# Attention products of a fused attention and two-expert-layer kernel, taken as 64x64 quarters of TensorE's array

## The chip, the cores and the metric

The kernel runs on one core of a Trainium2 chip. The metric is the device time of one execution in microseconds (us); the median of three runs of the kernel before is 707.98 us (705.53 to 710.4). The engines are named as in the profile: PE (TensorE matmuls), PEld (TensorE weight loads), DVE (VectorE), ACT (ScalarE), POOL (GpSimd) and SP (SyncE, which issues most DMAs).

## What is computed

Three stages follow one another: an attention with a decaying state, and two layers that send every token to one of eight experts. Only the first is touched by the change.

```python
f = 1.0 / (1.0 + np.exp(-f_logit))            # q, k, v, f_logit: (4, 8, 768, 48)
for t in range(S):
    state = f[:, :, t, :, None] * state + np.einsum('bhd,bhe->bhde', k[:, :, t], v[:, :, t])
    y[:, :, t] = np.einsum('bhd,bhde->bhe', q[:, :, t], state)
...
x = attn_out.transpose(0, 2, 1, 3).reshape(B * S, H * D)     # 3072 tokens of 384
x = _moe_ref(x=x, **moe_kwargs)                               # first expert layer, with a capacity
return _moe2_ref(x=x, **moe2_kwargs)                          # second expert layer
```

## The kernel before

**Tiles.** The 3072 tokens are cut into 24 tiles of 128 tokens, six to a batch. Within a tile the recurrence is turned into matrix products: cumulative sums of the log gates (`G`, L402) give growth and decay factors `eg` and `ei`, the queries and keys are scaled by them (`QT` L422, `KD` L424), and each half tile of 64 tokens needs a product of scores (`sc`, L444), a masked copy of them (`SC`, L449), an update of the 48x48 states of all heads (`kv`, L466, summed into `S` at L478, and scaled to the next tile's start at L487), and an output (`y`, L509) from the state and from the masked scores. The eight heads lie as four pairs: one head of a pair on partitions 0 to 63, the other on 64 to 127.

**How the products use the array.** The scores are 16 products a tile on two quarters of the array: rows 0 to 63 with output partitions 0 to 63, and rows 64 to 127 with 64 to 127. The state updates are 8 products a tile with all 128 rows and 64 output partitions, 96 columns wide: for the first half tile the values stand in a buffer `Vn` whose lower 64 partitions are a copy (`copy_v`, L372) and whose upper ones are zero. The output is 16 products a tile, again 128 rows by 64 output partitions and 96 columns, and needs its operands block-wise: ACT places the state into a buffer `RS` with zero blocks (`place`, L498 and L499), and `RV` holds the values in the same manner; half of it comes by two DMAs of its own (`load_vs`, 2 x 48 KB a tile, L367 and L368), the other half by copies on POOL and DVE (`copy_vs`, L379). Each product in fp32 shows as two weight loads and two matmuls in the trace, transposes as one.

**Order of the work.** A software pipeline is written as a table `STAGES` of (stage, lag): in iteration `it` each stage works on tile `it - lag`, in the order of the table, and each engine takes its instructions in that order. On PE a tile's turn is `G`, `sc`, `kv`, the transposes `xp` (of output rows, L530) and `kp` (of keys, L433), `y`, and the router logits `rt` (L260), with some steps of the router (L131 to L141, L266) at every third tile. After the loop the last tiles are written out by hand, with pieces of the first expert group (L1140, L1163) between them, up to the sorting of the experts by their counts, which begins with a product `ps` (L802). The expert layers follow.

**Buffers and loads.** PSUM has eight 2 KB banks: `sc` and the `tr` tiles (`G`, `kp`, `xp`) and `rt` have two buffers each, `kv` and `y` one. SP issues, a tile, `F` (gates, 192 KB), two halves of `X` (keys and queries, 192 KB each), `Vn` (192 KB) and the two `RV` loads, and besides the stores of output rows (582 KB at every third tile), some weights for the first expert (`raw`, 256 KB each) and two clears of tables. `gates` (L392, L393) is on ACT, `bound` (L386) clips the gates on DVE before it. POOL also subtracts split weights (L1026) and issues the scatters of the router (L273).

Of the kernel before, what the change touches and what calls it, by code (L numbers as in the profile page):

```python
# [9 lines left out]
F32 = mybir.dt.float32  # L10
# [5 lines left out]
ALU = mybir.AluOpType  # L16
# [6 lines left out]
DM = H * D  # L23
# [3 lines left out]
P = 128  # L27
# [172 lines left out]
def _route(*args, **kw):  # L200
# [14 lines left out]

STAGES = (
    ("place", 6),
    ("bound", 2),
    ("g_choose", 9),
    ("g_save", 13),  # L220
    ("sums", 3),
    ("rows", 7),
    ("warm", 0),
    ("load_v", 3),
    ("load_vs", 4),
    ("load_x", 0),
    ("copy_v", 4),
    ("scores", 4),
    ("masked", 4),
    ("expand", 3),  # L230
    ("updates", 5),
    ("copy_vs", 5),
    ("g_rank", 10),
    ("g_store", 10),
    ("g_copy", 8),
    ("gates", 2),
    ("rows_t", 7),
    ("factors", 3),
    ("rows_c", 7),
    ("keys_t", 4),  # L240
    ("output", 6),
    ("g_list", 13),
    ("states", 5),
    ("lead", 11),
    ("g_turn", 8),
# [59 lines left out]
def _attention(tc, env, fn, kq, vn, vs, x1, tab1, early, masks, first, side, after, first_group):  # L305
# [3 lines left out]
    with ExitStack() as ctx:  # L309
# [10 lines left out]
        mask = env.cs[:, C_MASK : C_MASK + 64].unsqueeze(1).to_broadcast([P, 8, 64])  # L320
# [4 lines left out]
        NVB = 3  # L325
        NXB = 4
        NRB = 3
# [4 lines left out]
        vbuf = [b1.tile([P, 2, DM], F32, name=f"Vn{i}") for i in range(NVB)]  # L332

        sbuf = [b1.tile([P, 2, 2, NPAIR * D], F32, name=f"RS{i}") for i in range(2)]
        rbuf = [b1.tile([P, 2, 2, NPAIR * D], F32, name=f"RV{i}") for i in range(NRB)]
# [6 lines left out]
        for vb in vbuf:  # L342
            nc.gpsimd.memset(vb[64:128, 0], 0.0)
        for r in rbuf + sbuf:
            nc.gpsimd.memset(r[0:64, :, 1, :], 0.0)
            nc.gpsimd.memset(r[64:128, :, 0, :], 0.0)
# [11 lines left out]
        def load_v(i):  # L358
            t = tiles[i]
            t.Vn = vbuf[i % NVB]  # L360
            nc.sync.dma_start(out=t.Vn[:, 1], in_=vn[i])

        def load_vs(i):

            t = tiles[i]
            t.RV = rbuf[i % NRB]
            nc.sync.dma_start(out=t.RV[0:64, 1, 0, :], in_=vs[i, 0])  # L367
            nc.sync.dma_start(out=t.RV[64:128, 0, 1, :], in_=vs[i, 1])  # L368

        def copy_v(i):  # L370
            t = tiles[i]
            nc.gpsimd.tensor_copy(out=t.Vn[0:64, 0], in_=t.Vn[0:64, 1])  # L372

        def copy_vs(i):

            t = tiles[i]
            for h in range(2):
                u = slice(h * 64, h * 64 + 64)
                (nc.vector if h else nc.gpsimd).tensor_copy(  # L379
                    out=t.RV[u, h, h].rearrange("p (a e) -> p a e", e=D),  # L380
                    in_=t.Vn[u, 1].rearrange("p (a h e) -> p a h e", h=2, e=D)[:, :, h],
                )
# [35 lines left out]
        def factors(i):  # L418
            t = tiles[i]
            t.QT = b4.tile([P, NPAIR, P], F32, name=f"QT{i}", tag="QT")  # L420
            t.KD = e2.tile([P, NPAIR, P], F32, name=f"KD{i}", tag="KD")
            nc.vector.tensor_tensor(out=t.QT, in0=t.X[:, 1], in1=t.eg, op=ALU.mult)  # L422
            step()
            nc.vector.scalar_tensor_tensor(  # L424
# [12 lines left out]
        def scores(i):  # L437
            t = tiles[i]
            sc = t.sc = p_2.tile([P, NPAIR, 2, 64], F32, name=f"sc{i}", tag="sc")
            for a in range(NPAIR):  # L440
                for h in range(2):
                    u = slice(h * 64, h * 64 + 64)
                    for q in (slice(0, 64), slice(64, 128)):
                        nc.tensor.matmul(sc[q, a, h], t.KD[q, a, u], t.QT[q, a, u], start=True, stop=True)  # L444
# [1049 lines left out]
def tile_attention_moe_moe(  # L1494
# [91 lines left out]
    with ExitStack() as mo:  # L1586
# [22 lines left out]
        def side(i):  # L1609
# [12 lines left out]
            if i == SNAP + 14:  # L1622
                M.index(g0)
# [178 lines left out]
```

## Time and profile before

| | |
|---|---|
| median of 3 runs | 707.98 us |
| profiled execution, its own time | 709.22 us |
| its span, first to last instruction | 707.4 us |
| PE busy | 676.5 us (96% of the span) |
| DVE, ACT, POOL busy | 409.8, 322.2, 361.2 us |
| mean granted TensorE clock | 0.991 |
| attention loop, from the sums of tile 4 to those of tile 23 | 25.31 to 143.95 us |
| sorting of the first layer's experts begins | 177.95 us |

The span is one execution seen by the profiler; 1.8 us of the execution's own time lie outside of it. A matmul's row gives when it started and a modelled end, so the pace of PE is read from start to start. A group's mean duration is not its pace: matmuls overlap.

### The profile page before, as it was taken

To read this page: it belongs to the slowest core of one execution; us is meant where nothing else is said; L and a number is where in the kernel's file an instruction comes from. 1 tells how busy PE (TensorE), PEld (TensorE's weight loads), DVE (VectorE), ACT (ScalarE), POOL (GpSimd) and SP (SyncE) were. 2 spreads that over 40 slices of the span, in tenths; PEclk is the share of its full clock that TensorE was granted. 3 is DMA by queue.
4 is the path that set the end of the run, shared out by engine and by line. 5 is a ranking of instruction groups with operands and counts; after the bars stand their busy time and mean duration, and the time that the engine had idled before them with its cause. 6 is when DMAs were issued, how large, how long until landed. Compare 5 with 4: busy or idle time off the path is not lost.

```text
span 707.4 us, 15778 instructions
## 1 busy us (share of the span) xinstructions
PE 676.5 (96%) x5775; PEld 619.0 (87%) x5778; DVE 409.8 (58%) x1024; ACT 322.2 (46%) x697; POOL 361.2 (51%) x389
## 2 busy tenths in 40 slices
PE   7989999989999999999999899989999999999995
PEld 4878788877898989989999899989998899999994
DVE  4767777866486555745546654456344455464641
ACT  5668777743353434344343433144334334354420
POOL 5233444454365546565473651456656464576621
PEclk9999999999999999999999999999999999999998
DMA  8899899532485545355473520275445354454300
GB/s 191 248 203 224 199 183 215 127 83 93 131 258 159 152 120 155 97 154 141 126 185 97 159 95 1 68 237 161 141 115 164 101 155 131 136 154 147 92 25 20
DMA packets 63273, 99.79 MB, mean 141 GB/s; under 512 B 16588, under 2 KB 32942, under 8 KB 63187
## 3 DMA queue, kind: packets, MB, share of 16 engines
q1 hardware_dynamic: 55507, 83.06, 44.0%
q0 software_dynamic: 7680, 15.64, 7.9%
q8 instruction: 47, 0.77, 0.5%
q14 instruction: 39, 0.32, 0.2%
HBM read 82.90 MB, written 16.60 MB: 141 GB/s over the span
## 4 chain that ended last, share of the span: by engine, by line
PE 72%; DVE 9%; DMA 8%; issue 5%; ACT 2%; POOL 1%; SPq 0%; DVEq 0%; POOLq 0%; ACTq 0%
PE hpm L1163 27%; PE ypm L1187 8%; PE ypm L1188 8%; PE ypm L1189 8%; DMA out_dram<-yr,tdm 6%; PE y L509 3%; PE G L402 3%; PE sc L444 3%; PE tpm L1140 2%; PE kv L466 1%; PE tym L926 1%; PE warm L629 1%; PE tym L1001 1%; PE ltm L260 1%; PE kp L433 1%
## 5 line engine op out<-in xcount | busy, mean ns | idle before, releaser
L1174 ACT ACTIVATE hhm<-hpm 128x288 fp32r<-128x288 f32 (+11 forms) x152 | 72.4, 477 | 184.0 <-PE hpm L1163 163.5
L1163 PE MATMUL hpm<-xhm,w0h 128*128 128x288 f32 (+11 forms) x456 | 155.2, 341 | 0.4 <-DVE hlm L1175 0.3
L1187 PE MATMUL ypm<-hhm,w1h 128*128 128x288 f32 (+11 forms) x456 | 153.9, 338 | 0.0
L1175 DVE SCALAR_TENSOR_TENSOR hlm<-hpm,hhm 128x288 fp32r<-128x288 f32 (+11 forms) x152 | 81.2, 536 | 120.9 <-ACT hhm L1174 92.6
L1188 PE MATMUL ypm<-hlm,w1h 128*128 128x288 f32 (+11 forms) x456 | 150.6, 330 | 0.0
L1163 PE MATMUL hpm<-xhm,w0l 128*128 128x288 f32 (+11 forms) x456 | 150.5, 331 | 0.0
L1189 PE MATMUL ypm<-hhm,w1l 128*128 128x288 f32 (+11 forms) x456 | 150.4, 330 | 0.0
L1163 PE MATMUL hpm<-xlm,w0h 128*128 128x288 f32 (+11 forms) x456 | 144.6, 331 | 0.0
L1026 POOL TENSOR_TENSOR w0l<-raw,w0h 128x512 fp32r<-128x512 f32 x64 | 81.9, 1296 | 57.9 <-ACT w0h L1025 57.5
L1026 POOL TENSOR_TENSOR w1l<-raw,w1h 128x512 fp32r<-128x512 f32 x64 | 82.1, 1295 | 41.5 <-ACT w1h L1025 40.6
L295 POOL DMA_INDIRECT xrm<-x,idcm x64 | 69.8, 1090 | 55.6 <-DVE valm L1021 34.0
L1163 PEld LDWEIGHTS hpm<-xhm,w0h 128*128 128x128 f32 x456 | 86.3, 189 | 3.6 <-DVE hlm L1175 1.0
L1187 PEld LDWEIGHTS ypm<-hhm,w1h 128*128 128x128 f32 x456 | 85.9, 188 | 2.8 <-issue 0.6
L1163 PEld LDWEIGHTS hpm<-xhm,w0l 128*128 128x128 f32 x456 | 86.4, 190 | 2.0
L1189 PEld LDWEIGHTS ypm<-hhm,w1l 128*128 128x128 f32 x456 | 85.9, 188 | 2.2
L1188 PEld LDWEIGHTS ypm<-hlm,w1h 128*128 128x128 f32 x456 | 86.0, 189 | 2.1
L1163 PEld LDWEIGHTS hpm<-xlm,w0h 128*128 128x128 f32 x456 | 85.2, 189 | 2.3
L273 POOL DMA_INDIRECT tab<-pos,sum x30 | 30.5, 1018 | 64.8 <-DVE sum L182 58.4
L1148 ACT CAST xhm<-tpm 128x336 fp32r<-128x336 f32 (+8 forms) x64 | 25.2, 435 | 72.1 <-PE tpm L1140 69.0
L1025 ACT CAST w0h<-raw 128x512 fp32r<-128x512 f32 x96 | 57.2, 616 | 0.1
L1025 ACT CAST w1h<-raw 128x512 fp32r<-128x512 f32 x96 | 56.7, 621 | 0.0
L1149 DVE TENSOR_TENSOR xlm<-tpm,xhm 128x336 fp32r<-128x336 f32 (+8 forms) x64 | 29.4, 493 | 42.1 <-ACT xhm L1148 41.2
(209 smaller groups left out, 1040.4 us busy)
## 6 DMA issues: line engine op xcount, KB each, us to landing
raw<-in_w_dram SPq DMA_DIRECT2D x192, 256.0 KB
X<-in_kq_dram SPq DMA_DIRECT2D x48, 192.0 KB
x<-xr SPq DMA_DIRECT2D x8, 582.0 KB
F<-in_fn_dram SPq DMA_DIRECT2D x24, 192.0 KB
Vn<-in_vn_dram SPq DMA_DIRECT2D x24, 192.0 KB
RV<-in_vs_dram SPq DMA_DIRECT2D x48, 48.0 KB
xrm<-x,idcm POOLq DMA_INDIRECT x64
tab<-fill SPq DMA_DIRECT2D x2, 480.0 KB
```

Of the source, the lines that this page charges most:

```text
L273: ins = tc.nc.gpsimd.indirect_dma_start(out=dst, out_offset=bass.IndirectOffsetOnAxis(ap=idx, axis=0), in_=src, in_offset=None, bounds_che ...
L295: nc.gpsimd.indirect_dma_start(out=dst, out_offset=None, in_=src, in_offset=bass.IndirectOffsetOnAxis(ap=idx, axis=0), bounds_check=bound, ...
L1025: nc.scalar.copy(out=hi, in_=raw)
L1026: eng.tensor_tensor(out=lo, in0=raw, in1=hi.bitcast(F32), op=ALU.subtract)
L1148: nc.scalar.copy(out=g.xh[:, :, s], in_=tp[:, :, :Pr])
L1149: nc.vector.tensor_tensor(out=g.xl[:, :, s], in0=tp[:, :, :Pr], in1=g.xh[:, :, s].bitcast(F32), op=ALU.subtract)
L1163: nc.tensor.matmul(hp[:, :N], w[:, c, fs], x[:, c, :N], start=(k == 0), stop=(k == len(parts) - 1))
L1174: nc.scalar.activation(hh[:, :N], hp[:, :N], AF.Relu)
L1175: nc.vector.scalar_tensor_tensor(out=hl[:, :N], in0=hp[:, :N], scalar=0.0, in1=hh[:, :N].bitcast(F32), op0=ALU.max, op1=ALU.subtract)
L1187: nc.tensor.matmul(g.yp[d][:, :N], w2h[:, fc, ds_], hh[:, :N], start=(fc == 0), stop=False)
L1188: nc.tensor.matmul(g.yp[d][:, :N], w2h[:, fc, ds_], hl[:, :N], start=False, stop=False)
L1189: nc.tensor.matmul(g.yp[d][:, :N], w2l[:, fc, ds_], hh[:, :N], start=False, stop=(fc == NFC - 1))
```

## The change

The three kinds of products are written as 64x64 quarters, and everything that only fed their block form is dropped. `load_vs`, `copy_v`, `copy_vs` and `place` are gone, with the buffers `RV`, `RS` and the memsets of their zeros. `output` becomes `output_s` (queries times state, read from `S` itself) and `output_i` (masked scores times values, read from `Vn` itself). The states are added in two instructions, and the scaling of the state and `bound` move from DVE to POOL. `factors` is split into `queries` and `keys`. In PSUM `sc` and `kv` now share one buffer of two banks, one bank for each half of the array's rows, and take it one after the other within a tile; `y` has two banks. The values get four buffers.

```diff
 def scores(i):
-    sc = t.sc = p_2.tile([P, NPAIR, 2, 64], F32, name=f"sc{i}", tag="sc")
+    t.sc = p_1.tile([P, 2, 512], F32, name=f"sc{i}", tag="sc")
     for a in range(NPAIR):
-        for h in range(2):
-            u = slice(h * 64, h * 64 + 64)
-            for q in (slice(0, 64), slice(64, 128)):
-                nc.tensor.matmul(sc[q, a, h], t.KD[q, a, u], t.QT[q, a, u], start=True, stop=True)
+        for h, q in enumerate(half):
+            for u in half:
+                nc.tensor.matmul(
+                    t.sc[u, h, a * 64 : a * 64 + 64], t.KD[q, a, u], t.QT[q, a, u], start=True, stop=True
+                )
...
 def updates(i):
-    t.kv = p_1.tile([P, NPAIR, 2, D], F32, name=f"kv{i}", tag="kv")
+    t.kv = p_1.tile([P, 2, 512], F32, name=f"kv{i}", tag="sc")
...
-            nc.tensor.matmul(
-                t.kv[q, a, 0:n], t.KT[:, a, q], t.Vn[:, 0:n, v0 : v0 + D], start=True, stop=True
-            )
+            for k, u in enumerate(half[:n]):
+                nc.tensor.matmul(
+                    t.kv[q, k, a * D : (a + 1) * D],
+                    t.KT[u, a, q],
+                    t.Vn[u, v0 : v0 + D],
+                    start=True,
+                    stop=True,
+                )
...
 def states(i):
-    nc.vector.tensor_tensor(
-        out=t.S[:, 1:n].rearrange("p h (a e) -> p h a e", a=NPAIR),
-        in0=t.kv[:, :, 0 : n - 1].rearrange("p a h e -> p h a e"),
-        in1=pair(t.S[:, 0]).unsqueeze(1).to_broadcast([P, n - 1, NPAIR, D]),
-        op=ALU.add,
-    )
-    step()
+    for k in range(2 if c < TPB - 1 else 1):
+        nc.vector.tensor_tensor(
+            out=t.S[:, k + 1], in0=t.kv[:, k, 0 : NPAIR * D], in1=t.S[:, k], op=ALU.add
+        )
+        step()
     if c < TPB - 1:
-        nc.vector.tensor_tensor(
+        nc.gpsimd.tensor_tensor(
             out=pair(S[:, 0]),
...
-def output(i, pool=p_1, tag="y"):
-    t.y = pool.tile([P, 512], F32, name=f"y{i}", tag=tag)
...
-                nc.tensor.matmul(
-                    t.y[u, 2 * a * D : (2 * a + 2) * D].rearrange("p (h e) -> p h e", h=2),
-                    t.SC[:, a, h] if k else t.QT[:, a, u],
-                    (t.RV if k else t.RS)[:, h, :, e],
-                    start=k == 0,
-                    stop=k == 1,
-                )
+def output_s(i, tag="y"):
+    t.y = p_1.tile([P, 2, 512], F32, name=f"y{i}", tag=tag)
+    for a in range(NPAIR):
+        e = slice(a * D, (a + 1) * D)
+        for h, q in enumerate(half):
+            for k, u in enumerate(half):
+                nc.tensor.matmul(t.y[u, h, e], t.QT[q, a, u], t.S[q, k, e], start=a == 0, stop=False)
+
+def output_i(i):
+    for a in range(NPAIR):
+        e = slice(a * D, (a + 1) * D)
+        for h in range(2):
+            v0 = (2 * a + h) * D
+            for u in half:
+                nc.tensor.matmul(
+                    t.y[u, h, e],
+                    t.SC[u, h, a],
+                    t.Vn[u, v0 : v0 + D],
+                    start=False,
+                    stop=a == NPAIR - 1,
+                )
...
 def bound(i):
-    nc.vector.tensor_scalar(out=t.F, in0=t.F, scalar1=FMIN, scalar2=None, op0=ALU.max)
+    nc.gpsimd.tensor_scalar(out=t.F, in0=t.F, scalar1=FMIN, scalar2=None, op0=ALU.max)
```

The table of stages is written anew: `bound` has lag 1, `output_s` and `output_i` lag 6, `rows` (the copy of `y` by ACT, L524 before, now from two banks) lag 6 in place of 7. The first group's rows are gathered a little earlier, and the part after the loop stands in another order.

On PE before, in the loop, from the sums of tile 14 on (the number behind a name is its tile; a row of 64x96 or 64x64 is one product on a part of the array):

```order
L402 MATMUL G14_1611<-cs_71,L0_190 128x128 x4
L444 MATMUL sc13_1624<-QT13_1558,KD13_1559 64x64 x16
L466 MATMUL kv12_1649<-Vn0_192,KT12_1574 64x96 x8
L530 MATMUL xp10_1663<-cs_71,xr9_1503 128x128 x3
L433 MATMUL kp13_1679<-cs_71,KD13_1559 128x128 x4
L509 MATMUL y11_1686<-RS1_196,QT11_1332 64x96 x2
L509 MATMUL y11_1686<-RV2_199,SC11_1417 64x96 x2
```

The last two rows stand four times, then the logits `rt` of tile 10 and the sums of tile 15. On PE of the changed kernel the same turn of the loop is this:

```order
L260 MATMUL rt9_1772<-xT9_1718,wg1s_72 32x128 x3
L480 MATMUL y11_1784<-S11_1570,QT11_1469 64x48 x16
L443 MATMUL kv12_1801<-Vn0_195,KT12_1699 64x48 x16
L407 MATMUL kp13_1826<-cs_71,KD13_1761 128x128 x4
L373 MATMUL G14_1833<-cs_71,L0_193 128x128 x4
L514 MATMUL xp10_1838<-cs_71,xr9_1645 128x128 x3
L490 MATMUL y11_1784<-Vn3_198,SC11_1639 64x48 x16
L418 MATMUL sc13_1871<-QT13_1721,KD13_1761 64x64 x16
```

The quarter products now stand in two blocks, `output_s` with `kv`, and `output_i` with `sc`; the logits stand between `sc` and the next `output_s`, well behind the transposes they need.

On DVE before, from the mask of tile 12's scores to the sum of tile 11's states (names with `5` are steps of the router):

```order
L449 TENSOR_TENSOR SC12_1530<-sc12_1513,cs_71 128x512
L153 RECIPROCAL xr3_839<-sea5_1453 128x3
L379 COPY RV2_199<-Vn2_194 64x192
L422 TENSOR_TENSOR QT13_1558<-X1_187,eg13_1533 128x512
L175 TENSOR_REDUCE sfa5_1561<-t6a5_1486 128x3
L424 SCALAR_TENSOR_TENSOR KD13_1559<-ei13_1534,X1_187 128x512
L156 TENSOR_TENSOR cum1_80<-cum1_80,oha5_1376 128x8
L538 COPY xT9_1565<-xp9_1554 128x384
L184 CAST sua5_1567<-sfa5_1561 128x3
L478 TENSOR_TENSOR S11_1484<-kv11_1538,S11_1484 128x192
```

On DVE of the changed kernel, from the same mask on:

```order
L425 TENSOR_TENSOR SC12_1758<-sc12_1741,cs_71 128x512
L156 TENSOR_TENSOR cum1_80<-cum1_80,oha5_1565 128x8
L398 SCALAR_TENSOR_TENSOR KD13_1761<-ei13_1714,X1_190 128x512
L184 CAST sua5_1763<-sfa5_1723 128x3
L459 TENSOR_TENSOR S12_1818<-kv12_1801,S12_1818 128x192
L156 TENSOR_TENSOR cum1_80<-cum1_80,oha5_1565 128x8
L459 TENSOR_TENSOR S12_1818<-kv12_1801,S12_1818 128x192
L156 TENSOR_TENSOR cum1_80<-cum1_80,oha5_1565 128x8
L522 COPY xT10_1847<-xp10_1838 128x384
```

The mask now frees the one buffer that `kv` of the same tile waits for, the keys follow it, the copy `xT` comes before the queries, and the copy into `RV` is gone.

## Rows read from the trace of the kernel before

**Rows 1.** The page: busy time, share and instructions of PE, DVE, ACT, POOL.

```profile
PE 676.5 (96%) x5775; PEld 619.0 (87%) x5778; DVE 409.8 (58%) x1024; ACT 322.2 (46%) x697; POOL 361.2 (51%) x389
```

**Rows 2.** The chain of waits in order of time: start, us, what.

```profile
25.31 1.10 PE G L402 x8
...
143.95 1.09 PE G L402 x8
...
177.95 0.53 PE ps L802
```

**Rows 3.** Timeline of PE, one tile: start, us, instructions, idle before.

```profile
50.78 0.42 PE L260 MATMUL rt<-xT,wg1s 128*32 128x128 f32 x6 [1.21 <-DVE xT L538]
51.13 1.16 PE L402 MATMUL G<-cs,L 128*128 128x128 f32 x8
52.22 1.15 PE L444 MATMUL sc<-QT,KD 64*64 64x64 f32 x32
53.30 0.88 PE L466 MATMUL kv<-Vn,KT 128*64 128x96 f32 x16
54.11 0.55 PE L530 MATMUL xp<-cs,xr 128*128 128x128 f32 x3
54.49 0.60 PE L433 MATMUL kp<-cs,KD 128*128 128x128 f32 x4
55.02 0.39 PE L509 MATMUL y<-RS,QT 128*64 128x96 f32 x4
...
56.56 0.42 PE L260 MATMUL rt<-xT,wg1s 128*32 128x128 f32 x6
```

**Rows 4.** Timeline of PE, the 48-column update of a batch's last tile.

```profile
84.27 0.67 PE L466 MATMUL kv<-Vn,KT 128*64 128x48 f32 x16
84.87 0.44 PE L530 MATMUL xp<-cs,xr 128*128 128x128 f32 x2
```

**Rows 5.** Timeline of PE in stretches of 0.05 and 0.07 us.

```profile
95.43 0.27 PE L444 MATMUL sc<-QT,KD 64*64 64x64 f32 x2
...
100.49 0.31 PE L260 MATMUL rt<-xT,wg1s 128*32 128x128 f32 x3
```

**Rows 6.** Stretches: us, busy by engine (instructions), clock, DMA share, GB/s.

```profile
core 0: us, PE busy (x) PEld busy (x) DVE busy (x) ACT busy (x) POOL busy (x), PEclk, DMA share, GB/s
25.00:50.00 25.00, 23.66 (x411) 20.01 (x408) 17.73 (x42) 18.03 (x39) 6.96 (x14) 1.00 0.99 225
75.00:100.00 25.00, 23.75 (x409) 20.08 (x411) 19.57 (x57) 18.42 (x41) 9.82 (x19) 1.00 0.93 194
100.00:125.00 25.00, 24.08 (x426) 20.71 (x423) 19.24 (x60) 18.95 (x42) 9.88 (x19) 1.00 0.95 216
125.00:144.00 19.00, 18.79 (x322) 15.87 (x322) 16.72 (x51) 15.06 (x33) 9.18 (x16) 1.00 0.49 118
144.00:178.00 34.00, 30.92 (x402) 26.02 (x403) 20.66 (x82) 13.63 (x32) 18.39 (x23) 0.95 0.32 90
```

**Rows 7.** Waits, 25 to 144 us: total us, times, longest.

```profile
PE rt L260 <- DVE xT L538: 3.6, 5, 1.2
```

**Rows 8.** Groups of DVE, ACT, POOL, 25 to 144 us: count, busy, mean ns, idle before.

```profile
L449 DVE TENSOR_TENSOR SC<-sc,cs 128x512 f32<-128x512 f32 x19 | 13.1, 690 | 20.8 <-PE sc L444 20.8
L478 DVE TENSOR_TENSOR S<-kv,S 128x384 f32<-128x384 f32 (+1 forms) x20 | 10.4, 518 | 0.1
L386 DVE TENSOR_SCALAR F<-F 128x384 f32<-128x384 f32 x19 | 8.4, 440 | 4.3 <-DMA F<-in_fn_dram 4.3
L487 DVE TENSOR_TENSOR S<-S,glast 128x192 f32<-128x192 f32 x17 | 7.1, 415 | 0.5
...
L498 ACT COPY RS<-S 64x384 f32<-64x384 f32 x20 | 10.2, 512 | 18.0 <-DVE S L478 17.3 <-DVE sua L184 0.8
...
L372 POOL COPY Vn<-Vn 64x384 f32<-64x384 f32 x19 | 10.3, 541 | 31.2 <-DMA Vn<-in_vn_dram 26.6 <-PE sc L444 2.9 <-PE y L509 1.7
L1026 POOL TENSOR_TENSOR w0l<-raw,w0h 128x512 fp32r<-128x512 f32 x6 | 7.6, 1270 | 6.4 <-ACT w0h L1025 6.4
```

More of the change, by code (lines that the diff above doesn't have):

```diff
@@ L216 @@
 STAGES = (
-    ("place", 6),
-    ("bound", 2),
+    ("g_save", 13),
+    ("load_v", 3),
+    ("load_x", 0),
+    ("g_copy", 8),
+    ("gates", 2),
+    ("bound", 1),
+    ("output_s", 6),
+    ("updates", 5),
     ("g_choose", 9),
-    ("g_save", 13),
-    ("sums", 3),
-    ("rows", 7),
+    ("states", 5),
     ("warm", 0),
[L224 to L232, printed above, removed]
+    ("keys_t", 4),
     ("g_rank", 10),
     ("g_store", 10),
-    ("g_copy", 8),
-    ("gates", 2),
+    ("sums", 3),
+    ("g_turn", 8),
     ("rows_t", 7),
-    ("factors", 3),
+    ("expand", 3),
     ("rows_c", 7),
-    ("keys_t", 4),
-    ("output", 6),
+    ("queries", 3),
+    ("output_i", 6),
+    ("scores", 4),
+    ("lead", 11),
+    ("masked", 4),
+    ("keys", 3),
+    ("rows", 6),
     ("g_list", 13),
-    ("states", 5),
-    ("lead", 11),
-    ("g_turn", 8),
     ("logits", 7),
@@ L302, in _gather1, with _attention @@
     )
-def _attention(tc, env, fn, kq, vn, vs, x1, tab1, early, masks, first, side, after, first_group):
+def _attention(tc, env, fn, kq, vn, x1, tab1, early, masks, first, side, after, first_group):
     nc = tc.nc
@@ L331, in _attention @@
         lbuf = [e1.tile([P, H, 64], F32, name=f"L{i}") for i in range(2)]
-        vbuf = [b1.tile([P, 2, DM], F32, name=f"Vn{i}") for i in range(NVB)]
-        sbuf = [b1.tile([P, 2, 2, NPAIR * D], F32, name=f"RS{i}") for i in range(2)]
-        rbuf = [b1.tile([P, 2, 2, NPAIR * D], F32, name=f"RV{i}") for i in range(NRB)]
+        vbuf = [b1.tile([P, DM], F32, name=f"Vn{i}") for i in range(NVB)]
         for lb in lbuf:
@@ L632, in _attention @@
             f.__name__: f
-            for f in (load_x, load_v, load_vs, copy_v, copy_vs, bound, gates, sums, expand, factors, keys_t, scores, masked, updates, states, place,
-                      output, rows, rows_t, rows_c, logits, g_copy, g_turn, g_choose, g_rank, g_store, g_save, g_list, warm, lead)
+            for f in (load_x, load_v, bound, gates, sums, expand, queries, keys, keys_t, scores, masked, updates, states,
+                      output_s, output_i, rows, rows_t, rows_c, logits, g_copy, g_turn, g_choose, g_rank, g_store, g_save, g_list, warm, lead)
         }
@@ L1130, in prep, with turn @@
         divide(g, j)
-    def turn(g, j, tag="tr"):
+    def turn(g, j, tp=None):
         Pr = g.Pr
@@ L1623, in side @@
                 M.index(g0)
+            if i == NTILE + 3:
+                for j in range(g0.J):
+                    M.gather(g0, j)
         def after(i):
```

171 lines of the change are left out of this document (72 added, 99 removed).

## Prediction

> **What bounds the kernel now.** First the busy shares: PE is busy for 676.5 of 707.4 us [rows 1], so a shorter time has to come from PE's own work or from its waits. Then the chain in order of time: in the attention loop the sums `G` of tile 4 start at 25.31 and those of tile 23 at 143.95 us, and the expert sorting begins at 177.95 [rows 2]. A tile of the loop therefore costs (143.95 - 25.31) / 19 = 6.24 us. Then the timeline of PE over one tile: from one start of `rt` to the next 56.56 - 50.78 = 5.78 us go by without an idle piece [rows 3]. The 0.46 us between 5.78 and 6.24 are waits; the one that the trace names is `rt` waiting for DVE's copy `xT`, up to 1.2 us at once [rows 3, 7]. Last the stretches of the loop: the DMA engines are busy for 0.93 to 0.99 of the time at 194 to 225 GB/s until 125 us, and for 0.49 after that, when the loads are in [rows 6]. So two resources are close to their limit in the loop, PE with 5.78 and the DMA engines with some 0.96 x 6.24 = 6.0 us a tile, and DVE and ACT are at 71 to 78%.
>
> The median of the runs shown, 707.98 us, lies 1.2 us below the profiled execution's 709.22. The sum below is made against 709.22 (the span and 1.8 us around it).
>
> **The products on PE.** From start to start, `sc` takes 53.30 - 52.22 = 1.08 us for 32 pairs of load and matmul [rows 3], and the 48-column `kv` takes 84.87 - 84.27 = 0.60 us for 16 pairs [rows 4]. Both run two pairs at once: two matmuls of `sc`, on two quarters, start within 0.05 us and last 0.27 each, and three of `rt`, on three column groups, start within 0.07 [rows 5]. So `sc` has 16 steps and this `kv` 8, a step costs (1.08 - 0.60) / 8 = 0.06 us, and 0.12 us are left for filling and the change of shape. 64 and 48 columns cost the same step.
>
> The change keeps `sc` at 32 pairs, makes 32 of `kv` in place of 16, and 64 of the output in place of 32. `output_s`, `kv` and `sc` use all four quarters in turn. `output_i` uses two: half tile u reads rows u and writes partitions u. No row shows four at once. Its bounds: all four overlap (8 steps, 0.015 us a pair), or two as now (16 steps, 0.03 us a pair). I take the first, because the rows show overlap between column groups that share all rows (`rt`) and between quarters that differ in both (`sc`), and starts that are far closer than a step [rows 5]. Then the two blocks cost:
> - `output_s` with `kv`: 16 x 0.06 + 0.12 = 1.08 us
> - `output_i` with `sc`: (16 + 8) x 0.06 + 0.12 = 1.56 us
>
> What else PE does for a tile stays as it is [rows 3]: `rt` 51.13 - 50.78 = 0.35, `G` 1.09, `xp` 54.49 - 54.11 = 0.38, `kp` 55.02 - 54.49 = 0.53, together 2.35. The sum is 2.35 + 1.08 + 1.56 = 4.99 us against 5.78. The output itself gains nothing, since 64 pairs in 24 steps replace 32 wider ones (56.56 - 55.02 = 1.54 us); the gain is in `sc` and `kv` and in two changes of shape fewer.
>
> One rule speaks against `output_i`. Its two row groups write the same bank at once, on different partitions. The Trainium skill, TensorEngine Tiling (Array Packing), section Restrictions and Gotchas, says that different row tiles cannot access the same PSUM bank simultaneously. The trace disagrees as far as it goes: `sc` before is one tile of 512 numbers a partition, its two row groups write it, and they run together [rows 5]. By the rule `output_i` would have 32 steps; that is a rival below.
>
> **The waits on PE.** `rt` now stands behind `output_i` and `sc`, 1.56 us after `xp`, and DVE copies `xT` before the queries, so the wait of rows 7 goes. Two waits come in. `kv` takes the buffer of `sc` when DVE has masked the scores (0.69 us [rows 8]); `rt` and `output_s` lie between, 0.35 + 0.60 = 0.95 us, so some 0.25 us are left for the two hand-overs. Behind `kv` in PE's queue stand `kp` and `G`, so a late mask delays the whole turn. And `output_s` waits until ACT has emptied the two banks of `y`, one copy of the former size, with `sc` and `rt` (0.48 + 0.35 us) for cover. I cost both at nothing; without cover each costs its own lateness, at most the 1.2 us of rows 7 a tile.
>
> **The other engines.** Per tile DVE loses `bound` (0.44) and the state's scaling (0.42) [rows 8]. The sum of states becomes two halves: between 0.26 each (half of 0.52) and 0.42 each (the row of that shape); I take 0.35, so 0.70 for 0.52. ACT loses `place`, two copies of 0.51 us. POOL loses the copy of `Vn` (0.54) with its waits for the DMA, and gains `bound` and the scaling, of 384 and 192 numbers a partition: no row has them; the copy of 384 gives 0.54 and the subtraction of 512 gives 1.27 as ends for the first, 0.27 and 1.27 for the second (the lower end again half of the copy), and I take 0.8 and 0.5, near the copy with some allowance for the second operand. POOL is busy for some 40% of the loop [rows 6], which hides this; if it were late, the next tile's states on DVE would be late by as much. In the first microseconds `bound` stands behind POOL's memsets; I leave that at nothing, between a loss of 2 us and a gain of 1 from memsets that go.
>
> **The DMA engines.** 6.24 us at the mean of the three rows, 212 GB/s [rows 6], are 1.32 MB a tile. The two `RV` loads are 2 x 64 x 768 bytes = 0.098 MB, 7.4%. If the engines do the rest in the same time per byte, a tile needs 6.0 x 0.926 = 5.55 us of them, more than PE's 4.99. The bytes may also go faster: 225 GB/s in one stretch, 194 in another at nearly the same share. I take 5.55 for the 16 tiles while the loads last, and 4.99 + 0.1 = 5.1 for the last three: (16 x 5.55 + 3 x 5.1) / 19 = 5.48 us a tile. The loop then gains 19 x (6.24 - 5.48) = 14.4 us.
>
> **After the loop.** From the last `G` to the sorting 34.0 us go by, 30.92 of them with PE busy [rows 2, 6]. In it stand two blocks of `sc` (0.48 us less each), two of `kv` (up to 0.21 less each), three outputs (up to 0.14 more each where `output_s` and `output_i` stand apart), and `place` (1.0 us) leaves the last tile's chain. That is 0.96 + 0.42 - 0.42 + 1.0 = 2.0 us. The code there is in another order, so I bound it: PE's idle time of 3.1 us and half of the work's gain make 4 us at best, three waits like that of rows 7 make 4 us of loss at worst.
>
> **Sum.** 709.2 - 14.4 - 2.0 = 692.8, so 693 us. The expert layers only start earlier.
>
> **Rivals.**
> - The DMA engines follow and PE sets the pace: 5.1 us a tile. For it speaks that the rate goes from 194 to 225 GB/s at nearly one share, so that the share is no fixed amount of work; against it, that the share is 0.93 to 0.99 already. 709.2 - 19 x 1.14 - 2 = 685.5 us. Chance 0.13.
> - New waits come on top: the mask, the copy of `y` and the loads each late now and then, with the old 0.46 us a tile added to 5.48. For it speaks that DVE is busy for 71 to 78% [rows 6] and takes its work strictly in order. 709.2 - 19 x 0.30 - 2 = 701.5 us, within 1% of before (700.9 to 715.1, about what a measurement can tell from no change). Chance 0.19.
> - Slower: the pace stays at two pairs a step, because quarters that share their output columns exclude each other or because PE is not fed faster than 0.03 us a pair. Place: `output_s`, `kv` and `sc`, 24 steps more, 1.44 us. A tile costs 6.43 us before any wait; with the 0.46, 6.89, without them 6.43. 709.2 + 19 x (0.19 to 0.65) = 713 to 722, middle 717 us. It decides from the point where a pair costs 0.015 + (6.24 - 4.99) / 96 = 0.028 us. Against it speak the starts of rows 5; for it, that no row shows more than two quarters of this size at once. Chance 0.12.
> - The bank rule holds for `output_i`: 16 steps more, 0.96 us; 4.99 + 0.96 + 0.3 = 6.25 us a tile, so about 709 - 2 = 707 us. Chance 0.04.
>
> **How the numbers follow.** The forecast, 687 to 699 with DMA-paced tiles, has the remaining 0.52. Faster by over 1%: the forecast, the first rival and a third of the second, 0.70. Within 1%: the rest of the second, the bank rule and a little of the slower one, 0.18. Slower: 0.12. The range 682 to 708 takes in the forecast, the first rival, the second and the bank rule's case.
>
> **What would show it.** Right: 32 pairs of `sc` in about 0.5 us from start to start, a tile near 5.5 us until the loads end and near 5.1 after, the DMA share near 1, hardly an idle piece ahead of `rt`. Wrong: `sc` still at about 1 us, or idle pieces ahead of `kv` that DVE's mask ends, or a DMA share well below 0.9 with tiles above 5.5 us, or a part after the loop of 34 us or more.

## The result, and the profile after

The changed kernel takes 712.27 us in the median (710.45 to 715.44, ten runs), the kernel before 709.62 in the same series. The ratio is 1.0059 (95% interval 1.0032 to 1.0086): a little slower, within 1%, 19 us above the forecast. The profiled execution took 715.44 us, the longest of the ten, 3.2 us above their median; its span is 713.6. The parts below are parts of that one execution.

The page: PE, DVE, ACT and POOL, to be set beside [rows 1].

```profile
PE 665.3 (93%) x6866; PEld 614.0 (86%) x6866; DVE 395.0 (55%) x972; ACT 299.2 (42%) x649; POOL 380.0 (53%) x376
```

PE has 11 us less work in 6 us more time. The chain of waits in order of time (start, us, what) tells where, against [rows 2].

```profile
15.40 5.15 DMA F<-in_fn_dram
...
20.62 1.16 POOL F L357
21.79 0.21 POOL S L457
...
22.02 0.37 DVE S L459
...
22.83 0.69 PE sc L418 x32
...
32.26 0.89 PE G L373 x8
...
154.10 0.89 PE G L373 x8
...
184.89 0.05 PE ps L781
```

- Start, up to the sums of tile 4: 32.26 - 25.31 = 6.95 us more (forecast: none).
- Loop, to the sums of tile 23: 121.84 us against 118.64, 3.2 us more, 6.41 us a tile for 6.24 (forecast: 14.4 us less).
- After the loop, to the sorting: 30.79 us against 34.00, 3.2 us less (forecast: 2.0 less).
- From the sorting on: 528.7 against 529.5 us.

The timeline of PE over one tile in which nothing stops it, against [rows 3]:

```profile
54.71 0.42 PE L260 MATMUL rt<-xT,wg1s 128*32 128x128 f32 x6
55.06 0.68 PE L480 MATMUL y<-S,QT 64*64 64x48 f32 x32
55.60 0.68 PE L443 MATMUL kv<-Vn,KT 64*64 64x48 f32 x32
56.22 0.66 PE L407 MATMUL kp<-cs,KD 128*128 128x128 f32 x4
56.71 1.06 PE L373 MATMUL G<-cs,L 128*128 128x128 f32 x8
57.60 0.49 PE L514 MATMUL xp<-cs,xr 128*128 128x128 f32 x3
58.02 1.07 PE L490 MATMUL y<-Vn,SC 64*64 64x48 f32 x29
...
58.99 0.65 PE L418 MATMUL sc<-QT,KD 64*64 64x64 f32 x30
59.57 0.42 PE L260 MATMUL rt<-xT,wg1s 128*32 128x128 f32 x6
```

From `rt` to `rt` it is 4.86 us, where the forecast had 4.99. `output_s` with `kv` takes 56.22 - 55.06 = 1.16 (1.08 forecast), `output_i` with `sc` 59.57 - 58.02 = 1.55 (1.56). So four quarters do run at once, and PE's work was forecast rightly. What is lost in the loop are stops. The waits on PE between 32 and 154 us (total, times, longest):

```profile
PE kp L407 <- DVE KD L398: 8.4, 8, 1.9
PE sc L418 <- issue: 2.7, 2, 1.9
PE kv L443 <- DVE SC L425: 2.4, 3, 0.9
PE sc L418 <- DVE S L459: 2.0, 1, 2.0
```

And the stretches (columns as in [rows 6]): two of 25 us, two chosen around dips of the clock, and the whole loop:

```profile
25.00:50.00 25.00, 21.89 (x588) 18.72 (x584) 14.62 (x36) 14.18 (x31) 11.31 (x19) 0.99 0.97 223
50.00:75.00 25.00, 23.70 (x622) 21.31 (x620) 15.74 (x43) 15.25 (x35) 9.27 (x15) 0.95 0.60 161
...
97.10:107.30 10.20, 8.35 (x146) 7.62 (x145) 5.93 (x14) 2.38 (x5) 5.09 (x8) 0.50 0.91 149
49.30:52.70 3.40, 3.40 (x25) 3.31 (x22) 0.52 (x2) 1.54 (x5) 0.00 (x0) 0.50 0.44 119
...
32.26:154.10 121.84, 105.42 (x2829) 93.31 (x2829) 79.09 (x210) 68.97 (x152) 65.26 (x85) 0.93 0.68 158
```

In the loop the granted clock is 0.50, the lower of the two levels (1.2 GHz), in three stretches: 3.4 us from 49.3, 10.2 from 97.1 and 3.4 from 141.5 us; the kernel before has none there. Each begins 2.9 to 3.6 us after the start of a stop of PE of 1.8 to 2 us (from 45.76, 93.99 and 138.61 us). Half of the busy time in them, 1.7 + 4.2 + 1.7 = 7.6 us, is lost. The account of the loop: 19 tiles of 4.86, some 0.15 us a tile for the router's products at every third tile, 16.4 us of waits (the four rows above and three of 0.3) and 7.6 of half clock make 119 of the 121.8 us; the rest has no name.

Three kinds of stop stand behind the waits. First, the keys. POOL and DVE at one of the eight places:

```profile
60.28 1.27 POOL L1005 TENSOR_TENSOR w0l<-raw,w0h 128x512 fp32r<-128x512 f32 x1 [1.63 <-ACT w0h L1004]
61.53 1.61 POOL L357 TENSOR_SCALAR F<-F 128x384 f32<-128x384 f32 x1
...
59.72 0.69 DVE L425 TENSOR_TENSOR SC<-sc,cs 128x512 f32<-128x512 f32 x1 [0.24 <-PE sc L418]
...
60.41 1.69 DVE L398 SCALAR_TENSOR_TENSOR KD<-ei,X 128x512 f32<-128x512 f32 x1
```

The keys take 0.68 us alone and 1.69 here: they end 0.55 us after POOL's subtraction does, so they moved little while it ran. The clipping behind it takes 1.61 us instead of 1.17. The mask, which reads PSUM, keeps its 0.69 us beside a subtraction (one on POOL from 83.99 us, 1.28 long):

```profile
84.40 0.69 DVE L425 TENSOR_TENSOR SC<-sc,cs 128x512 f32<-128x512 f32 x1 [1.22 <-PE sc L418]
```

The Trainium skill, SBUF — State Buffer, section SBUF: two separate sides, says that DVE and GpSimd share a pair of ports under an exclusive lock, which a DVE operation with two SBUF operands takes against a GpSimd operation that reads SBUF. These rows agree; a clipping and keys that start together at 99.8 us do not, for they take 1.21 and 1.06 us side by side, so neither is blocked for the whole of the other. Before, these subtractions stood beside the sums of states, the mask and small steps of the router, and the keys took 0.68 us at nearly every tile (two of twenty took more, 1.03 and 0.87).

Second, POOL's order. The end of the wait near 94 us, on POOL, DVE and PE:

```profile
91.36 1.08 POOL L273 DMA_INDIRECT tab<-tokid,sua  x1 [3.05 <-DVE sua L184]
92.74 0.97 POOL L273 DMA_INDIRECT tab<-tokid,sua  x1 [0.30 <-PE G L373]
93.74 1.21 POOL L357 TENSOR_SCALAR F<-F 128x384 f32<-128x384 f32 x1
94.86 0.28 POOL L457 MEMSET S<- 128x192 f32 x1
...
95.18 0.36 DVE L459 TENSOR_TENSOR S<-kv,S 128x192 f32<-128x192 f32 x1 [4.11 <-POOL S L457]
...
95.98 0.69 PE L418 MATMUL sc<-QT,KD 64*64 64x64 f32 x32 [1.99 <-DVE S L459]
```

The change also moved the clearing of a batch's first state (L457) from DVE to POOL, which I had passed over and which "The change" does not name. It stands behind two scatters and the clipping; DVE's sum waits for it, and with it the bank that `sc` takes over from `kv`. The chain above shows the same at the start: the clipping waits for the load of tile 4, and the first state of all waits behind it.

Third, stops in the middle of a block, with nothing named:

```profile
45.23 0.53 PE L418 MATMUL sc<-QT,KD 64*64 64x64 f32 x16
47.67 0.45 PE L418 MATMUL sc<-QT,KD 64*64 64x64 f32 x14 [1.91 <-issue]
```

Behind 18 of the block's 32 matmuls PE stands. In the records of the DMA engines a block of 16 KB of instructions (queue q8) lands at 46.07 us, and PE goes on 1.60 us later. That PE waits for these instructions is an inference from such pairs of times.

### The profile page after: what moved, and what is told of

Same layout as the page of the kernel before. It is cut to its first block, busy times and chain, and to the rows that moved or that the text cites. A ratio compares the mean times of both kernels' runs of the same rounds, so it can differ in the third digit from the quotient of the medians.

```text
span 713.6 us, 17703 instructions
## 1 busy us (share of the span) xinstructions
PE 665.3 (93%) x6866; PEld 614.0 (86%) x6866; DVE 395.0 (55%) x972; ACT 299.2 (42%) x649; POOL 380.0 (53%) x376
## 3 DMA queue, kind: packets, MB, share of 16 engines
q1 hardware_dynamic: 51667, 80.70, 41.5%
## 4 chain that ended last, share of the span: by engine, by line
PE 76%; DVE 9%; DMA 8%; issue 4%; POOL 2%; ACT 1%; SPq 0%; POOLq 0%; DVEq 0%; ACTq 0%
PE hpm L1145 27%; PE ypm L1169 9%; PE ypm L1170 9%; PE ypm L1171 9%; DMA out_dram<-yr,tdm 6%; PE G L373 3%; PE y L490 3%; DMA F<-in_fn_dram 2%; PE tpm L1121 2%; DVE KD L398 2%; PE kp L407 2%; PE sc L418 2%; PE tym L905 2%; PE xp L514 1%; PE tym L980 1%
## 5 line engine op out<-in xcount | busy, mean ns | idle before, releaser
L1145 PE MATMUL hpm<-xhm,w0h 128*128 128x288 f32 (+11 forms) x432 | 147.9, 343 | 0.3 <-DVE hlm L1157 0.3
L1156 ACT ACTIVATE hhm<-hpm 128x288 fp32r<-128x288 f32 (+11 forms) x144 | 69.6, 483 | 179.0 <-PE hpm L1145 173.7
L1157 DVE SCALAR_TENSOR_TENSOR hlm<-hpm,hhm 128x288 fp32r<-128x288 f32 (+11 forms) x144 | 78.1, 543 | 119.9 <-ACT hhm L1156 119.6
L1145 PE MATMUL hpm<-xhm,w0l 128*128 128x288 f32 (+11 forms) x432 | 143.9, 334 | 0.0
L1145 PE MATMUL hpm<-xlm,w0h 128*128 128x288 f32 (+11 forms) x432 | 138.2, 333 | 0.0
L1145 PEld LDWEIGHTS hpm<-xhm,w0h 128*128 128x128 f32 x432 | 81.8, 189 | 3.0 <-DVE hlm L1157 0.5
L1145 PEld LDWEIGHTS hpm<-xhm,w0l 128*128 128x128 f32 x432 | 81.9, 190 | 2.0
L1145 PEld LDWEIGHTS hpm<-xlm,w0h 128*128 128x128 f32 x432 | 80.9, 189 | 2.3
L273 POOL DMA_INDIRECT out_dram<-yr,tdm x34 | 35.8, 1054 | 33.6 <-DVE yr L981 28.0
```

The costliest lines, as they stand in the source:

```text
L273: ins = tc.nc.gpsimd.indirect_dma_start(out=dst, out_offset=bass.IndirectOffsetOnAxis(ap=idx, axis=0), in_=src, in_offset=None, bounds_che ...
L1145: nc.tensor.matmul(hp[:, :N], w[:, c, fs], x[:, c, :N], start=(k == 0), stop=(k == len(parts) - 1))
L1156: nc.scalar.activation(hh[:, :N], hp[:, :N], AF.Relu)
L1157: nc.vector.scalar_tensor_tensor(out=hl[:, :N], in0=hp[:, :N], scalar=0.0, in1=hh[:, :N].bitcast(F32), op0=ALU.max, op1=ALU.subtract)
```

## The experiments

All edits are made to the changed kernel. A ratio is that of a run's times to those of the kernel before in the same series.

**One part at a time (first series).** Run e1: the split of weights at another place.

```diff
                 if 0 <= it - lag < NTILE:
                     locals_[nm](it - lag)
-            after(it)
+                if nm == "gates":
+                    after(it - 1)
+        after(NTILE + 2)
```

> The changed kernel with the splitting of the expert weights (ACT's copy and POOL's subtraction, 1.28 us each in its trace) moved from the end of an iteration to just behind the gates of the next one, nothing else. Theory 1: the changed kernel lost its gain to DVE, whose keys and queries stand still while POOL subtracts weights (keys 1.0 to 2.5 us where nothing is beside them 0.68), so that the key transposes on PE wait 8.4 us in the loop. Then the keys stay at 0.7 to 1.0 us, the waits for them fall below 4 us, and the time goes from 712 to about 704 to 707 us. Theory 2: the loss comes from the PE clock, which falls by itself under quarter products: five or six stretches at half clock stay, and the time is 710 to 713 us. Theory 3: the waits are set by POOL's clipping of the gates and its place in POOL's order, not by the subtraction: 710 to 713 us with the longest waits still behind POOL's memset of a state.

Measured: 708.1 us, ratio 1.0007 (0.9976 to 1.0038), 4 us better than the changed kernel had been. That compares two series, and the intervals of the two ratios overlap a little (1.0032 to 1.0038); within its own series e1 lies clearly below e2 and e4 (1.0082 and 1.0088), each the changed kernel with another edit. Its waits on PE between 32 and 146 us:

```profile
PE kv L443 <- DVE SC L425: 2.6, 4, 0.9
PE sc L418 <- issue: 2.3, 2, 1.4
PE kp L407 <- DVE KD L398: 2.2, 2, 1.9
PE sc L418 <- DVE S L459: 2.0, 1, 2.0
```

The keys' wait fell from 8.4 to 2.2 us, and the loop from 121.8 to 113.4 us, 5 us shorter than before the change: theory 1 holds for this part. The total gains nothing on the kernel before, since the sums of tile 4 start at 32.2 us, 7 us later than there. Only two tiles of the loop still have keys of about 1 us (1.06 and 1.02). From 49 to 70 us four tiles in a row take 5.0 to 5.2 us each. The stretches of e1:

```profile
25.00:50.00 25.00, 22.71 (x590) 19.54 (x590) 13.47 (x34) 14.41 (x32) 8.94 (x17) 0.98 0.85 196
50.00:75.00 25.00, 24.36 (x744) 21.56 (x746) 18.01 (x49) 16.72 (x38) 15.54 (x20) 1.00 0.67 171
```

So tiles at PE's pace leave the DMA engines free for a third of the time. The share adds up the times of all packets over 16 engines. From the start to the sorting, and over the loop, before and then changed:

```profile
0.00:178.00 178.00, 165.69 (x2599) 137.05 (x2603) 125.22 (x364) 116.14 (x254) 77.48 (x145) 0.99 0.77 176
25.31:143.95 118.64, 113.87 (x1967) 96.75 (x1967) 90.89 (x257) 88.94 (x194) 46.58 (x86) 1.00 0.89 196
...
0.00:185.00 185.00, 154.76 (x3689) 131.68 (x3689) 110.57 (x311) 92.67 (x206) 97.05 (x134) 0.94 0.65 158
```

To the sorting that is 0.77 x 178 = 137 us of DMA work before and 0.65 x 185 = 120 in the changed kernel: 12% less for 7% fewer bytes (31.3 and 29.2 MB). In the changed loop 0.68 x 121.84 = 83 us are left, 4.4 a tile, well below PE's 5.0; the forecast had 5.55. A part of this is that 19.3 MB move in this loop for 23.3 in the one before, as more loads are in when it starts, 7 us later.

Run e2: `nc.vector` for `nc.gpsimd` in `bound`. Run e3: the same in the scaling of the state as well. Run e4: `("warm", 0)` behind `("sums", 3)` in the table.

> The changed kernel with the clipping of the gates back on DVE (0.44 us there before, 1.17 us and more on POOL now), at the same place of the order. Theory 3, that POOL is late for the state's memset and scaling because it clips first: the wait of 4.1 us for the memset near 94 us shrinks to under 2, the first tiles start 1 to 3 us earlier, and the time is 706 to 709 us. Theory 1 alone, that the weights' subtraction is what hurts: the keys stay at 1.6 us beside a subtraction and the time changes by under 2 us, 710 to 712. A rival: DVE now waits in order for the gates' load ahead of the sums of states, and the time is 713 us or more.

Measured: 712.36 us, ratio 1.0082 (1.0051 to 1.0113). The longest wait for the memset near the middle of the loop fell from 4.1 to 2.6 us, but the sums of tile 4 still start at 32.0 and the keys' mean stays at 1.02 us: beside a subtraction from 57.49 us, with no clipping left on POOL, they again take 1.69. Moving the clipping alone gains nothing; the subtraction is what stretches the keys.

> As the run with the clipping on DVE, and the scaling of the state back on DVE too (0.42 us there, 0.51 us on POOL). If the state's way through POOL holds the chain of states (POOL queue behind scatters of 1 us each and subtractions of 1.3), 1 to 3 us less than that run: 704 to 707 us. If the scaling is hidden on POOL, the 0.4 us a tile on DVE show as 0 to 3 us more than that run.

Measured: 717.02 us, ratio 1.0139 (1.0110 to 1.0168), 5 us worse than e2, more than the 0 to 3 expected. Here the scaling was better off on POOL; e8 and g4 below, which move it in other company, show no difference clear of noise (1.6 us each way).

> The changed kernel with the filler products on PE (11, 7 and 3 of them in three of the first iterations) behind the transposes of the keys and the sums of the gates, where they stood ahead of them. If the first tiles are late (sums of tile 4 at 32.1 us for 25.3 before) because the sums of tile 2 stand behind 4.2 us of filler, these start 3 to 4 us earlier and the sums of tile 4 at 28 to 29 us: 708 to 709 us in all. If the loads of the gates and POOL's clipping of them set the start, the sums of tile 4 stay at 31 to 32 us and the time at 711 to 713.

Measured: 713.55 us, ratio 1.0088 (1.0057 to 1.0119); tile 2's sums start at 14.8 instead of 19.3 us, those of tile 4 at 31.0, some 1 us earlier. The filler alone isn't the cause of the late start.

**POOL's order (second series, on top of e1).** Run e5 puts the memset back on DVE; e6 also moves `("bound", 1)` behind `("states", 5)`; e7 is e6 with e4's edit, e8 is e6 with the scaling on DVE.

```diff
-                nc.gpsimd.memset(t.S[:, 0], 0.0)
+                nc.vector.memset(t.S[:, 0], 0.0)
```

> The run with the splitting of the weights moved, and the memset of a batch's first state back on DVE (four instructions in all). In that run this memset stands on POOL behind scatters and the clipping of the next gates: DVE waits 6.6 us for it in the first tiles and 4.1 us near 91.9 us, and the scores' bank, which DVE's sums of states free, keeps PE waiting 3.4 and 2.0 us. If this is what makes the first tiles late, the sums of tile 4 start at 26 to 28 us (32.2 there), tile 14 takes 8 us or less (10.6), and the time is 700 to 703 us. If the load of the gates sets the start anyway, the sums of tile 4 stay at 31 to 32 us and the time is 706 to 708.

> As the run before with the memset on DVE, and POOL's clipping of the gates behind the scaling of the state in the order of an iteration, no longer ahead of it. If POOL's order still holds the chain of states (clipping 1.17 to 1.6 us ahead of the scaling), 1 to 3 us less: 698 to 701. If the scaling was hidden, the same time within 1 us, or a little more, because the clipped gates come later to ACT.

> As the run with memset and clipping moved, and the filler products on PE behind the transposes of the keys and the sums of the gates. With the wait for the memset gone, filler is what stands ahead of the sums in the first tiles (4.2, 1.7 and 0.8 us): the sums of tile 4 start 1 to 3 us earlier, the time falls by as much. If the loads set the start, nothing.

> As the run with memset and clipping moved, and the scaling of the state back on DVE. If the scaling is on the path on POOL (behind scatters), 1 to 3 us less than that run. If it is hidden there, the 0.4 us a tile that DVE does more stand between the sums of states and the queries: 0 to 3 us more.

Measured: e5 707.05 us (ratio 0.9990, 0.9963 to 1.0016), e6 706.78 (0.9985, 0.9960 to 1.0010), e7 708.15 (1.0004, 0.9966 to 1.0043), e8 708.34 (1.0004, 0.9963 to 1.0046). The four can't be told apart, nor from before. DVE no longer waits for POOL's memset, and the sums of tile 4 start at 29.6, 30.2, 28.1 and 33.2 us (32.2 in e1). None reaches the 698 to 703 us that e5 and e6 would have had if POOL's order had been all; as expected for hidden parts, e6 to e8 lie within 1.6 us of each other. Other stops come up: in the profiled execution of e6 PE stands for 5.57 us within `kv`. At 714.31 us it is the longest of ten (median 706.78), so this stop is no measure of the others. PE there, and the DMA queues from 98 to 110 us (packets, MB, share of 16 engines; as packets' times add up, it can exceed 100%):

```profile
103.37 0.59 PE L443 MATMUL kv<-Vn,KT 64*64 64x48 f32 x14
109.53 0.77 PE L443 MATMUL kv<-Vn,KT 64*64 64x48 f32 x18 [5.57 <-issue]
```

```profile
q1 hardware_dynamic: 1838, 2.36, 109.8%
...
q8 instruction: 1, 0.02, 0.7%
```

One block of instructions was sent in these 12 us; the one before it had landed at 97.96. It landed at 107.96, and PE went on 1.57 us later. Five such stops, in three traces, end 1.42 to 1.63 us behind a landing. A tile of the changed kernel has 298 loads and matmuls on PE for 202 before, and 22 such blocks are sent in its loop for 16 before. In this trace every stop of 1.7 us or more in the loop (from 43.1, 80.8 and 104.0 us) is followed by a stretch at half clock, 20.5 us together. Such stops take back gains; that they are the whole reason why the gains don't add up isn't shown.

**All moves, and the clears (third series).** f1 is e8 with e4's edit. f2 adds larger pieces for the two table clears, f5 is the changed kernel with these alone:

```diff
-    env.fill = cp.tile([P, E * RC // P // 4], I32, name="fill")
+    env.fill = cp.tile([P, E * RC * TW // P // 2], I32, name="fill")
```

> All moves so far together: the splitting of weights moved, memset of the state and its scaling on DVE, the clipping on POOL behind the states, the filler behind the sums. If the gains found one by one add up, the sums of tile 4 start near 28 us and the loop takes 112 to 115 us: 701 to 705 us in all. If each only uncovers the next wait, 706 to 708 as the single ones.

> As the run with all moves, and the two clears of tables (480 KB each in pieces of 240 bytes) written in pieces of 1920 bytes. Theory: PE stops in the middle of a block (3.5 to 5.6 us near 97 to 104 us) because the block of its own instructions, 16 KB, comes late through DMA engines that the clear keeps busy; the half clock behind the stop costs about as much again. Then the stop near 97 us goes or falls below 1 us, and the time is 3 to 7 us less than that run. Rival: the stop belongs to PE and its instructions whatever the DMA engines do: it stays at 3 us or more and the time within 1.5 us.

> The changed kernel itself with only the clears of tables in pieces of 1920 bytes. If late instructions are a part of its loss apart from the other waits, 2 to 4 us less than the changed kernel: 708 to 710 us. If its own waits near 94 us cover the late instructions there, no difference: 711 to 713.

Run f4 is f2 with the scatters (`g_list`) one iteration later; the list of the first expert's tokens is then read at 127.2 us, before a scatter at 130.8 that belongs ahead of it, so a part of the list is missing and f4 does not do the same work.

> As the run with all moves and the clears in larger pieces, and the scatters of the router behind the clipping in POOL's order, one iteration later in the table. POOL's subtraction of weights no longer waits behind two scatters: the queries that it holds (1.6 to 2.2 us in three tiles) come back to 0.7 us, PE's waits of 0.7 to 1.3 us for the mask go, and the time is 1 to 4 us less than without this move. If the scatters now hold the clipping and with it the gates, it is the same or more.

Measured: f1 724.63 us (ratio 1.0195, 1.0167 to 1.0223), f2 718.25 (1.0104, 1.0068 to 1.0139), f4 714.30 (1.0063, 1.0033 to 1.0093), f5 723.56 (1.0206, 1.0169 to 1.0244). Between f1 and f2 lie the 6 us expected of the clears: in one trace each, the waits of `kv` without a named releaser go from 6.0 to 2.1 us, that of `sc` (3.6 us) is gone. That speaks for instructions held up by DMA traffic, but by one pair of runs only, and f5, expected at 708 to 713 us, gained nothing. f4 is 4 us below f2, as expected, with its part left out. All but f4 lose far more than their parts did in the second series (f1 was expected at 701 to 708 us), and f1, f2 and f5 show what no earlier trace had shown: ACT stands still for some 2 us.

**Repeats (fourth and fifth series).** g1 is the changed kernel, g2 is f2, h1 is the kernel before, all unchanged. In g3 two subtractions of f2 move by an iteration (13 and 19 in `SPLITS` become 14 and 20); g4 is g3 with the scaling on POOL; h2 is g3 with the second clear in its old pieces.

> The changed kernel once more, unchanged, as the measure for this series. If the series before was special: 711 to 714 us, ratio to before 1.004 to 1.009, and ACT without stops of 2 us. If chips differ in how late instructions come: a ratio above 1.01 with ACT stops in its trace.

> The run with all moves and the clears in larger pieces once more, unchanged (718 us before, with two ACT stops of 2 us in the loop and 17 us at half clock in the part after it). If those belonged to the series: 697 to 703 us, the loop from tile 4 to 23 in 108 to 112 us. If they belong to the code: 715 to 719 again.

> As that run, with two of the twelve subtractions of weights moved by one iteration, off the iterations in which POOL has two scatters to send first. The queries are no longer held there (1.6 to 2.2 us, 0.7 without): 1 to 3 us less than that run. If other work on POOL takes the place of the subtraction beside the queries: the same within 1 us.

> As the run with the subtractions moved, but with the scaling of the state on POOL, as in the changed kernel. If the scaling is hidden on POOL: the same time or up to 2 us less, since DVE has 0.4 us a tile less to do. If it stands behind scatters there and is late: 1 to 3 us more.

> The kernel before once more, unchanged, for its trace in this series. If the series is like the last two: ACT stops of 1.5 to 2 us stand in its trace too if they belong to the chip's way of handing out ACT's instructions, at other places, and its waits on PE hide them; or none are there and they belong to the changed program. Its time against itself: ratio 0.997 to 1.003.

> All moves, two subtractions moved off the scatters, and larger pieces in the first clear alone (the second, with larger pieces, went along with 3 us more between the expert layers). In a series without ACT stops: 697 to 703 us, faster than before by 1%. In one with them: 712 to 717 us, ratio to before 1.003 to 1.009.

Measured: g1 721.62 us (ratio 1.0173, 1.0149 to 1.0198), g2 721.88 (1.0148, 1.0106 to 1.0190), g3 718.54 (1.0109, 1.0083 to 1.0134), g4 720.09 (1.0163, 1.0109 to 1.0218); h1 710.84 (1.0009, 0.9981 to 1.0036), h2 727.86 (1.0230, 1.0199 to 1.0262). The same changed kernel is 0.6% slower than before in one series and 1.7% in another; the kernel before stays at 708 to 711 us in all. The record names a chip for each of the five series of experiments, and each time another one (6, 4, 15, 5, 3; none for the series of the result), so what goes with a series may go with its chip; no run separates the two. ACT and PE of g1, at one of the stops:

```profile
107.64 0.52 ACT L364 ACTIVATE L<-En 128x384 f32<-128x384 f32 x1
110.58 0.58 ACT L409 COPY KT<-kp 128x512 f32<-128x512 f32 x1 [2.42 <-PE G L373]
...
108.02 0.66 PE L407 MATMUL kp<-cs,KD 128*128 128x128 f32 x4
...
111.22 0.55 PE L514 MATMUL xp<-cs,xr 128*128 128x128 f32 x3 [1.65 <-ACT KT L409]
```

The product that the copy `KT` needs has its modelled end at 108.68, and ACT was free at 108.16; it began 1.90 us later. In the trace's semaphore records the count that this copy waits for, which PE raises at the ends of its products, goes up at 110.50 and 110.56 us, and the copy starts at 110.58. So by these records (569 of the count's 590 updates are there) it is PE's signal that is late, not ACT; why it is late no run shows. The copy of tile 16 is late by 1.5 to 2.0 us in f1, f2, f5 and g1 to g4, that of tile 22 in these and h2. Neither the first trace of the changed kernel nor those of e1 to e8, f4 and h1 have it, and f4 is the one run of the last three series with a version of the changed kernel below 1.01.

These stops in the loop are the smaller part of the loss. The profiled executions in parts, by the starts of PE's matmuls (us):

| run | start to the sums of tile 4 | loop | to the sorting | from there on |
|---|---|---|---|---|
| before | 25.2 | 118.6 | 33.9 | 529.6 |
| h1, before again | 27.6 | 118.1 | 32.7 | 529.3 |
| changed | 32.1 | 121.9 | 30.8 | 528.9 |
| e1 | 32.2 | 113.4 | 33.4 | 527.5 |
| e8 | 33.2 | 112.1 | 31.3 | 530.1 |
| f2 | 27.4 | 113.3 | 40.2 | 536.2 |
| g1, changed again | 30.2 | 117.6 | 36.3 | 531.8 |
| g3 | 28.6 | 114.3 | 41.5 | 535.2 |

In the last three series most of these loops are shorter than the one before the change; what is lost lies behind them. Two waits of g1 there, on ACT and on PE:

```profile
ACT xr L505 <- remote: 6.3, 1, 6.3
...
PE xp L514 <- ACT xr L505: 3.7, 1, 3.7
```

This copy `xr` of an output stands for 6.3 to 6.5 us, and PE behind it for 3.3 to 3.7, in every trace of the last three series but h1, and PE for 0.2 at most in the changed kernel's first trace and in those of e1 to e8. In g1 it starts at 165.69 us, again just behind PE's signal (165.67; the product's modelled end is 162.22), and 10.2 us at half clock follow the stop's start. From the sorting on, the seven runs with larger pieces for a clear take 534.7 to 536.5 us and all others 527.4 to 532.7. The second clear alone is not the reason, for h2, which has its old pieces there, takes 536.5; what is, no run shows.

g3 is 3 us better than g2, as expected, but their intervals overlap; h2 is 10 us above both of its cases, which stays unexplained. No version beats the kernel before by more than the noise.

## Why the prediction was wrong

Against the forecast of 692.8 us the profiled execution is 22.6 us late: 7.0 of them in the start, 17.7 in the loop (121.8 us for 19 x 5.48 = 104.1), less 1.2 after it and 0.8 from the sorting on. The loop's part is the sum of two errors of opposite sign: PE's own pace of 5.0 us a tile instead of the 5.48 of the DMA engines (9 us less), and waits and half clock that the sum had at nothing (24 us more, and 2.6 without a name).

- **PE's work: right.** 4.86 us a tile for 4.99 forecast, `output_s` with `kv` 1.16 for 1.08, `output_i` with `sc` 1.55 for 1.56. The slower rival's mechanism (two pairs a step) falls. So does the bank rule of the Trainium skill, TensorEngine Tiling (Array Packing), section Restrictions and Gotchas, as far as `output_i` goes: two row groups write one bank, on different partitions, and the block takes no step more; by the rule it would be 2.5 us instead of 1.55. That the times of these two rivals, 713 to 722 and 707 us, lie closer to the measured one than the forecast does is chance.
- **New waits on PE: the step that failed.** "I cost both at nothing" was said of the mask and the copy of `y`, and no third wait was counted. The loop has 16.4 us of waits, of which the mask costs 2.4 and the copy of `y` none; the keys behind it, on which `kp` waits, cost 8.4. I did not see them, though the rows of DVE's order before and after show `KD` moved behind the mask, next to the end of an iteration where the subtractions stand. The rival of new waits named the right kind and 0.46 us a tile, 9 us; with 7.6 us of half clock behind them they come to 24.
- **"POOL is busy for some 40% of the loop, which hides this": wrong.** The clipping was taken at 0.8 us and measures 1.17 alone and 1.34 in the mean (the scaling 0.51, as taken); POOL is busy for 65.26 of 121.84 us, 54%. But its length isn't the point, as e2 shows: a share says nothing of the order and the shared port. POOL's queue holds scatters that wait, so the memset behind them is late, and its subtractions, which stood on POOL before the change too, stop the keys at their new place.
- **The DMA engines as the bound: wrong.** Tiles of 5.0 to 5.2 us stand beside a share of 0.67, so a share near 1 in the loop before was no limit of 5.55 us a tile. "If the engines do the rest in the same time per byte" is off by some 5% (12% less work for 7% fewer bytes). Alone this error would have made the time shorter than forecast, near the rival of 685.5 us.
- **The start: bounds too narrow.** 6.95 us against "a loss of 2 us and a gain of 1". In e5, with the memset off POOL, 2.6 us come back against e1, and in e7, with the clipping and the filler moved as well, 4.1; in e8 nothing does, with a stop of 2.1 us in `kv` ahead of these sums. The rest is open.
- **After the loop: right.** 3.2 us less for 2.0 forecast.

What is shown: PE's pace, the missing DMA bound, the keys beside the subtractions (in e1 the wait goes and the loop is 8 us shorter), the wait for the memset (its going in e5 was seen, a gain in time was not). What is shown in traces but not by an edit of its own: the half clock behind stops. What is argued from times that go together: the late instructions. What stays open: most of the late start, the further 1.1% in the last three series and the loss behind the loop there, the late signals of PE, and with them whether the moves together would have brought the forecast.

## What to carry to other kernels

When an engine's own work shrinks, take each of its waits as a new candidate and read the queue in front of whoever ends it; a busy share of 40% is no proof that work is hidden, since it says nothing of the order in the queue. Before an operation with two SBUF operands goes to a new place, look at what GpSimd does at that moment. In this loop a stop of PE of about 2 us cost more than double, since a stretch at half clock followed each of the three (5.8 us of stops, 7.6 of half clock). And divide a total into its stages before judging a part: e1 made the loop 5 us shorter than before, and a start 7 us later hid it.

## What the runs showed that I had not expected

- The DMA engines' busy time doesn't quite go with bytes: to the sorting, 137 us fell to 120, 12%, when two loads of 48 KB a tile in pieces of 768 bytes, 7% of the bytes, were left out.
- PE stops in the middle of a block with no releaser named, 1.91 us in the changed kernel and 5.57 in e6, each stop ending some 1.6 us behind the landing of a 16 KB block of instructions.
- In g1, PE's signal on which two of ACT's copies wait is recorded 1.8 and 3.5 us behind the modelled end of the product. Such copies come late in nearly all traces of the last three series and in none of the earlier ones.
- A clipping that takes 0.44 us on DVE took 1.17 us on POOL with nothing beside it, and 1.20 to 1.66 us beside the keys or queries.
- One program on one core can differ by 1.1% against another between series, which may also differ in the chip (ratio 1.0059 and 1.0173), where each series alone has an interval of 0.3%.
